# Routing over eleven steps, gate weights written with the last heads' rows, and another split of the opening, in a fused attention and expert kernel

## The chip, the cores and the metric

One core of one Trainium2 chip runs the whole program. The time is device microseconds of one launch; below, us means that. TensorE, VectorE (DVE), ScalarE (ACT), GpSimd (POOL) and SyncE (SP, which issues most DMAs) run in parallel, each with its own queue of instructions in program order, and wait for each other by semaphores.

## What is computed

Attention over 4 batches, 8 heads, 576 tokens and 64 dimensions, a mixture of 8 experts with one expert per token, and a gated feed-forward layer, all in float32:

```python
q_rot, k_rot = rotate(q), rotate(k)                      # rotary positions
scores = q_rot @ k_rot.T / 8                             # 32 heads of 576 x 576
attn = exp(scores - max); attn /= sum(attn) + 1e-9
x = (attn @ v).transpose(0, 2, 1, 3).reshape(2304, 512)
logits = x @ w_gate                                      # 8 experts
e = argmax(logits); gate_w = softmax(logits)[e]
eom = sigmoid(x @ w_output_gate)[e]
x = gate_w * eom * (relu(x @ w1[e]) @ w2[e])
out = (sigmoid(x @ g) * (x @ v2)) @ o                    # 512 -> 1536 -> 512
```

## The kernel before

The program has three stages: attention with routing (0 to about 360 us), the experts (to about 656 us) and the feed-forward layer (to the end). Each float32 operand of a large matmul is split into an upper half (rounded) and a lower half (the rest), and three products are added.

**Attention** works on 16 pairs of heads, g = 0 to 15, four pairs to a batch, and each pair takes five steps j = 0 to 4 of 128 query rows (the last step of 64). The step counter is t = 5g + j. The order of the work is written out by hand in one loop: a step issues `scores(t)` on TensorE, row maxima (L274) on DVE and exponentials (L281) on ScalarE, then the products with v of step t-2, the transposes of the probabilities of step t-1, and parts of the work for other pairs:

- `rot(g, nm)` rotates queries or keys of a pair: part `a` is three products, part `b` the sum. The pair is rotated two pairs ahead, on GpSimd, in steps 0, 1 (`a`) and 3, 4 (`b`). Pair 0 is rotated on DVE. For pair 1, GpSimd makes the products and DVE the sums, in steps 2 and 3 of pair 0.
- `tqk(g)` transposes what was rotated and splits it into halves, one pair ahead, in steps 0 (keys), 1 (queries) and 2 (the 64 last tokens, `tails`); the halves are made on DVE.
- `xf(g)` in steps 3 and 4 transposes the result of pair g-1, divides it by the row sums (tile `x`), makes the pair's part of the logits (tile `lh`) and writes the rows to `x_dram` through SP's queue (L390, L393).
- `load(g+3)`, in step 4, queues the next loads of q, k and v on SP.

**Routing.** When a batch's four pairs are through, `route(b)` returns seven lists of small operations, and the loop runs one list per step, from the step after `xf` of the last pair: logits summed over the eight heads, maximum, one-hot of the first maximum, positions by small matmuls with a triangular matrix, a scatter of token numbers to `perm_dram` by five indirect DMAs on GpSimd (`scatter`), and the gate weight `den`, which goes to column 512 of `x_dram`, one float to a row. For batches 0 to 2 this lies beside the attention of the next pairs; for batch 3 the operations are placed by hand between the first experts' matmuls. After batch 2, `slots(False)` computes a table of which expert takes which rows: 23 small operations on DVE, five to a step. At t = 75 the first experts' weights and rows are loaded (`load_w`, `gather`).

Of the kernel before, what the change touches and what calls it, by code (L numbers as in the profile page):

```python
# [9 lines left out]
F32 = mybir.dt.float32  # L10
# [33 lines left out]
XW = DM + 1  # L44
# [20 lines left out]
def tile_kernel(  # L65
# [60 lines left out]
    pp = pool(att_a, "pp", 3)  # L126
    ptp = pool(att_a, "ptp", 3)
    per = pool(att_a, "per", 1)
    xp = pool(att_a, "xp", 2)
    sm = pool(att_a, "sm", 8)  # L130
    rt = pool(att_a, "rt", 1)
    qkt = pool(att_q, "qkt", 1)
# [77 lines left out]

        return a, b

    def tqk(g):
        i = g % 2

        def halves_of(hi, lo, ps, nm):

            f = SCALE if nm == "q" else 1.0
            nc.vector.tensor_scalar(out=hi, in0=ps, scalar1=f, scalar2=None, op0=ALU.mult)
            nc.vector.scalar_tensor_tensor(  # L220
                out=lo, in0=ps, scalar=f, in1=hi.bitcast(F32), op0=ALU.mult, op1=ALU.subtract
            )

        def main(nm):
            def f():
                src = rotd[g, nm]
                h, l = qT[i] if nm == "q" else (t[:, 64:576] for t in kT[i])
                ps = pst.tile([128, 512], F32, tag="t", name="t")
                for c in range(4):
                    nc.tensor.transpose(ps[:, 128 * c : 128 * c + 128], src[:, c, :], idf)  # L230
                halves_of(h, l, ps, nm)

            return f

        def tails():
            ps = pst.tile([128, 512], F32, tag="t", name="t")
            for n, nm in enumerate("kq"):
                nc.tensor.transpose(ps[:, 64 * n : 64 * n + 64], rotd.pop((g, nm))[0:64, 4, :], idf[0:64, 0:64])
            for c in (0, 576):
                halves_of(*(t[:, c : c + 64] for t in kT[i]), ps[:, 0:64], "k")  # L240
            for e in range(2):
                r = slice(64 * e, 64 * e + 64)
                halves_of(*(t[r, r] for t in qD[i]), ps[r, 64:128], "q")

        return [main("k"), main("q"), tails]
# [96 lines left out]

    def xf(g):
        b, h = divmod(g, 4)
        l = lsum[b % 2][:, :, 2 * h : 2 * h + 2]
        st = {}

        def part(c0, nch):  # L350
            def f():
                if c0 == 0:
                    st["r"] = sm.tile([128, 5, 2], F32, tag="r", name="r")
                    st["x"] = xp.tile([128, 5, 128], F32, tag="x", name="x")
                    sp = sm.tile([128, 2], F32, tag="sp", name="sp")
                    nc.vector.tensor_tensor(out=sp, in0=halves, in1=lst.pop(g).to_broadcast([128, 2]), op=ALU.mult)
                    st["sp"] = sp
                X, r = st["x"], st["r"][:, c0 : c0 + nch, :]
                ps = pst.tile([128, 512], F32, tag="t", name="t")
                for c in range(nch):  # L360
                    cc = c0 + c
                    nc.tensor.matmul(
                        ps[:, 160 * c : 160 * c + 160],
                        O[g % 2][:, 128 * cc : 128 * cc + 128],
                        wI[:, h, :],
                        start=True,
                        stop=True,
                    )
                if c0:
                    nc.tensor.matmul(ps[:, 320:322], fold, st["sp"], start=True, stop=True)  # L370
                    nc.vector.tensor_copy(l[:, 4, :], ps[:, 320:322])
                nc.vector.tensor_scalar(out=r, in0=l[:, c0 : c0 + nch, :], scalar1=EPS, scalar2=None, op0=ALU.add)
                nc.vector.reciprocal(out=r, in_=r)
                r = r.unsqueeze(3)
                pv_ = ps[:, 0 : 160 * nch].rearrange("p (c w) -> p c w", w=160)
                nc.vector.tensor_tensor(
                    out=lh[:, c0 : c0 + nch, 2 * h : 2 * h + 2, :],
                    in0=pv_[:, :, 128:160].rearrange("p c (e w) -> p c e w", e=2),
                    in1=r.to_broadcast([128, nch, 2, 2 * E]),
                    op=ALU.mult,  # L380
                )
                nc.vector.tensor_tensor(
                    out=X[:, c0 : c0 + nch, :].rearrange("p c (e d) -> p c e d", e=2),
                    in0=pv_[:, :, 0:128].rearrange("p c (e d) -> p c e d", e=2),
                    in1=r.to_broadcast([128, nch, 2, D]),
                    op=ALU.mult,
                )
                if c0:
                    t0, hc = b * S + 1, slice(128 * h, 128 * h + 128)
                    nc.sync.dma_start(  # L390
                        out=x_dram[t0 : t0 + 512, hc].rearrange("(p c) d -> p c d", c=4), in_=X[:, 0:4, :]
                    )
                    nc.sync.dma_start(out=x_dram[t0 + 512 : t0 + 576, hc], in_=X[0:64, 4, :])  # L393

            return f

        return [part(0, 3), part(3, 2)]
# [11 lines left out]
    def route(b):  # L409
# [4 lines left out]
        def logits():  # L414
            st["lg"] = lg = t3("lg", 2 * E)
            st["L"] = lg[:, :, 0:E]
            nc.vector.tensor_reduce(out=lg, in_=lh.rearrange("p c h e -> p c e h"), axis=AX.X, op=ALU.add)

        def top():
            st["mx"] = t2("mx")  # L420
# [93 lines left out]

        def weight():
            den = st["den"]
            nc.vector.reciprocal(out=den, in_=den)
            t0 = b * S + 1
            nc.sync.dma_start(
                out=x_dram[t0 : t0 + 512, DM : DM + 1].rearrange("(p c) d -> p (c d)", c=4), in_=den[:, 0:4]  # L520
            )
            nc.sync.dma_start(out=x_dram[t0 + 512 : t0 + 576, DM : DM + 1], in_=den[0:64, 4:5])

        return [
            [logits, top, at_top],
            [first, first_max, onehot],
            [before],
            [place, own, own_sum],
            [scatter, gate],
            [gate_sum, guard, both],  # L530
            [weight],
        ]

    def scatter_group(ins, b, c):
# [430 lines left out]
    for nm in "kq":  # L965
        for f in R[nm]:
            f(eng=nc.vector)
    first = tqk(0)
    first[0]()
    first[1]()  # L970
    first[2]()
    load(2)
    second = {nm: rot(1, nm) for nm in "kq"}
    for nm in "kq":
        second[nm][0]()

    def late_setup():
        nc.sync.dma_start(out=mc, in_=misc)
# [36 lines left out]
    for t in range(NJ * NPAIR):  # L1015
        g, j = divmod(t, NJ)
        if t == NJ * (NPAIR - 1):
            att_b.close()
            open_moe()
            M["table"], M["later"], M["ids"], M["want"] = False, [], 0, FRONT  # L1020
            more_ids()
            for i in range(NPC):
                load_w(0, i)
            gather(0)
            gather(1)
        scores(g, j)
        if t >= 2:
            pv(*divmod(t - 2, NJ))
        if t >= 1:
            turn_last(*divmod(t - 1, NJ))  # L1030
        if g >= 1 and j in (3, 4):
            if j == 3:
                xs_ = xf(g - 1)
            xs_[j - 3]()
        if g == 0:
            if j == 2:
                tq = tqk(1)
                second["k"][1](nc.vector)
                tq[0]()
            elif j == 3:  # L1040
                second["q"][1](nc.vector)
                tq[1]()
            elif j == 4:
                tq[2]()
        elif g + 1 < NPAIR and j < 3:
            if j == 0:
                tq = tqk(g + 1)
            tq[j]()
        if t >= 1:
            turn(*divmod(t - 1, NJ))  # L1050

        n = g + 2
        if n < NPAIR:
            if j == 0:
                ahead[n] = rot(n, "k"), rot(n, "q")
                ahead[n][0][0]()
            elif j == 1:
                ahead[n][1][0]()
            elif j == 3:
                ahead[n][0][1]()  # L1060
            elif j == 4:
                ahead.pop(n)[1][1]()
                if g + 3 < NPAIR:
                    load(g + 3)
        if t == 2:
            late_setup()
        if t == 5:
            late_setup2()
        if j == 4 and g >= 4 and g % 4 == 0:
            for n, fs in enumerate(route(g // 4 - 1)):  # L1070
                plan.setdefault(t + 1 + n, []).extend(fs)
            if g == NPAIR - 4:
                it = iter(slots(False))
                for n in range(5, 10):
                    plan.setdefault(t + n, []).extend(islice(it, 5))
                plan[t + 10] = list(it)
        for f in plan.pop(t, []):
            f()
        if g == NPAIR - 1 and j in (2, 3):
            take(1)  # L1080
# [237 lines left out]
```

## Time and profile before

| | |
|---|---|
| median of 3 runs | 1150.48 us (1150.36 to 1151.25) |
| profiled execution, own time | 1141.22 us |
| its span, first to last instruction | 1139.5 us |
| TensorE busy | 1074.9 us, 94% of the span |
| DVE, ScalarE, GpSimd busy | 68%, 51%, 30% |
| mean granted TensorE clock | 0.985 of full speed |

The span is that of one execution under the hardware profiler. Busy shares are averages over the three stages; matmuls are pipelined, so that a busy TensorE isn't one at its peak. Timeline rows give the start, the duration, the engine, the source line, the operation, the tiles (out<-in), and in brackets the idle time of the engine before it with what ended that.

### The profile page before, as it was taken

Reading aid. Unit: us, or ns where it says so; the run is one execution under the profiler, and the core shown is the slowest. Engines: PE = TensorE matmul, PEld = TensorE weight load, DVE = VectorE, ACT = ScalarE, POOL = GpSimd, SP = SyncE. Lnnn points to the kernel's source line nnn. Section 1 sums busy time; section 2 is a strip of 40 time slices with the busy share of each in tenths; the row PEclk is TensorE's granted clock in tenths of the full one; section 3 lists DMA queues with packets and bytes.
Section 4 is the critical chain, followed back from the end, with each engine's and each line's share of the span. In section 5 each row is a group of like instructions: output and inputs, shape, how many; then the busy total and the mean of one; then the engine's idle time right before and its main releaser. Section 6 shows DMA issues by size and latency. Waiting matters only on the chain. (4 is left out here: it accounts for less than half of the span.)

```text
span 1139.5 us, 20624 instructions
## 1 busy us (share of the span) xinstructions
PE 1074.9 (94%) x7644; PEld 960.6 (84%) x7644; DVE 774.7 (68%) x1450; ACT 581.5 (51%) x1116; POOL 343.8 (30%) x324
## 2 busy tenths in 40 slices
PE   4999899889999999999999998899999999999998
PEld 3788788768778988887988887789999999999997
DVE  6878787768876887788888678864454444545442
ACT  2566466446554345566667455644443444444442
POOL 3636356353612213332224044521111111111111
PEclk9999899889999999999999999899999999999999
DMA  3132162144107396789999425310010010100000
GB/s 110 37 83 44 43 84 44 43 43 85 43 16 220 56 193 217 231 291 307 296 307 310 145 79 191 112 56 1 1 56 1 1 57 1 56 1 1 28 1 28
DMA packets 99485, 111.61 MB, mean 98 GB/s; under 512 B 19249, under 2 KB 77873, under 8 KB 99378
## 3 DMA queue, kind: packets, MB, share of 16 engines
q1 hardware_dynamic: 94914, 97.81, 31.0%
q0 software_dynamic: 4320, 12.08, 3.4%
q8 instruction: 62, 1.02, 0.4%
q10 hardware_dynamic: 144, 0.33, 0.1%
q14 instruction: 45, 0.37, 0.1%
HBM read 103.03 MB, written 15.56 MB: 104 GB/s over the span
## 5 line engine op out<-in xcount | busy, mean ns | idle before, releaser
L1202 POOL TENSOR_TENSOR gl<-gf,gh 128x384 fp32r<-128x384 f32 x72 | 73.1, 1015 | 350.9 <-ACT gh L1201 350.9
L281 ACT ACTIVATE p<-s,nm 128x576 f32<-128x576 f32 x144 | 105.5, 737 | 133.8 <-DVE nm L274 131.7
L746 DVE TENSOR_TENSOR lo<-wr,hi 128x1024 fp32r<-128x1024 f32 x112 | 150.4, 1359 | 17.8 <-ACT hi L745 17.4
L1198 DVE TENSOR_TENSOR gf<-v,sg 128x384 f32<-128x384 f32 x72 | 39.9, 554 | 138.6 <-PE v L1194 138.6
L274 DVE TENSOR_REDUCE nm<-s 128x1 f32<-128x576 f32 x144 | 102.9, 751 | 39.0 <-PE s L268 26.0
L1180 DVE TENSOR_TENSOR gl<-gw,gh 128x512 fp32r<-128x512 f32 x72 | 73.5, 1021 | 68.9 <-ACT gh L1179 68.9
L1201 ACT CAST gh<-gf 128x384 fp32r<-128x384 f32 x72 | 36.9, 513 | 161.6 <-DVE gf L1198 161.6
L745 ACT CAST hi<-wr 128x1024 fp32r<-128x1024 f32 x106 | 109.5, 1052 | 4.2 <-PE y L836 2.8
L1192 PE MATMUL t<-yh,gh 128*128 128x384 f32 x288 | 100.4, 349 | 6.7 <-ACT sg L1196 5.8
L1194 PE MATMUL t<-yh,gl 128*128 128x384 f32 x288 | 99.0, 344 | 4.1 <-DVE gl L1180 4.1
L314 PE MATMUL t<-idf,p 128*128 128x128 f32 x576 | 83.5, 280 | 18.6 <-DVE pt L300 16.2
L1193 PE MATMUL t<-yl,gh 128*128 128x384 f32 x288 | 98.2, 341 | 0.0
L1192 PE MATMUL v<-yh,vh 128*128 128x384 f32 x288 | 96.6, 335 | 0.0
L1193 PE MATMUL v<-yl,vh 128*128 128x384 f32 x288 | 96.5, 335 | 0.0
L1194 PE MATMUL v<-yh,vl 128*128 128x384 f32 x288 | 96.4, 335 | 0.0
L317 ACT COPY pt<-t 128x512 f32<-128x512 f32 x144 | 79.1, 588 | 32.9 <-PE t L314 32.1
L314 PEld LDWEIGHTS t<-idf,p 128*128 128x128 f32 x576 | 66.2, 145 | 24.9 <-DVE pt L300 20.5
L1216 PE MATMUL o<-oh,gl 128*128 128x512 f32 x216 | 86.2, 399 | 0.0
L1215 PE MATMUL o<-ol,gh 128*128 128x512 f32 x216 | 85.3, 395 | 0.0
L1214 PE MATMUL o<-oh,gh 128*128 128x512 f32 x216 | 84.0, 389 | 0.0
L805 PE MATMUL h<-xl,hi 128*128 128x256 f32 x288 | 82.0, 285 | 1.7 <-DVE sc L781 1.7
L805 PE MATMUL h<-xh,hi 128*128 128x256 f32 x288 | 81.9, 284 | 0.7 <-issue 0.7
(218 smaller groups left out, 2890.2 us busy)
## 6 DMA issues: line engine op xcount, KB each, us to landing
wr<-in_moe_w_dram SPq DMA_DIRECT2D x112, 512.0 KB
cv<-in_moe_w_gate_dram SPq DMA_DIRECT2D x12, 512.0 KB
cv<-in_moe_w_val_dram SPq DMA_DIRECT2D x12, 512.0 KB
cv<-in_moe_w_out_dram SPq DMA_DIRECT2D x12, 512.0 KB
yt<-y_dram SPq DMA_DIRECT2D x18, 256.0 KB
out_dram<-ob SPq DMA_DIRECT2D x18, 256.0 KB
kraw<-in_k_dram SPq DMA_DIRECT2D x16, 256.0 KB
qraw<-in_q_dram SPq DMA_DIRECT2D x16, 256.0 KB
```

Of the source, the lines that this page charges most:

```text
L274: nc.vector.tensor_reduce(out=nm, in_=s[:, :, 0:288], axis=AX.XY, op=ALU.max, negate=True)
L281: nc.scalar.activation(out=P[g, j][:, e, :].rearrange("p (a b) -> p a b", a=2), in_=s[:, :, 0:288], func=AF.Exp, bias=nm, scale=1.0, accum ...
L314: nc.tensor.transpose(ps[:, 128 * c : 128 * c + 128], src[:, e, k0 + 128 * c : k0 + 128 * c + 128], idf)
L745: nc.scalar.copy(out=hi, in_=t)
L746: nc.vector.tensor_tensor(out=lo, in0=t, in1=hi.bitcast(F32), op=ALU.subtract)
L805: nc.tensor.matmul(ps[:, c, :], w[:, kk, 128 * c : 128 * c + 128], x[:, kk, :], start=first, stop=last)
L1192: nc.tensor.matmul(ps[:, 0:TG], wh[:, c], yh[:, kk, :], start=(kk == 0), stop=False)
L1193: nc.tensor.matmul(ps[:, 0:TG], wh[:, c], yl[:, kk, :], start=False, stop=False)
L1194: nc.tensor.matmul(ps[:, 0:TG], wl[:, c], yh[:, kk, :], start=False, stop=(kk == KD - 1))
L1214: nc.tensor.matmul(ps, gh[:, c], wh, start=(f == 0), stop=False)
L1215: nc.tensor.matmul(ps, gh[:, c], wl, start=False, stop=False)
L1216: nc.tensor.matmul(ps, gl[:, c], wh, start=False, stop=(f == NF - 1))
```

## The change

Five things change.

- The opening: the upper halves of pair 0 are made on ScalarE; TensorE runs 30 transposes of the identity ahead of the keys' transposes and 8 ahead of the queries', into the same PSUM tile. GpSimd copies one element of the rotated queries before it starts on pair 1, and makes pair 1's sums as well.
- For batches 0 to 2 the sum over heads is made by three adds on GpSimd instead of one reduction on DVE.
- `route` returns eleven lists instead of seven, and the first runs in the step of `xf` itself, one step earlier than before.
- The table's operations come six to a step, from the step after `place`.
- The rows of a batch's last pair are kept (tile `x` has three buffers and a 129th column) until the gate weight is there, and rows and weight are written together, 129 columns wide.

```diff
-    xp = pool(att_a, "xp", 2)
+    xp = pool(att_a, "xp", 3)
...
-    def tqk(g):
+    def tqk(g, eng=nc.vector, spin=(0, 0, 0)):
         i = g % 2
+        def place(n):
+            ps = pst.tile([128, 512], F32, tag="t", name="t")
+            for _ in range(spin[n]):
+                nc.tensor.transpose(ps[:, 0:128], idf, idf)
+            return ps
...
-            nc.vector.tensor_scalar(out=hi, in0=ps, scalar1=f, scalar2=None, op0=ALU.mult)
+            if eng is nc.scalar:
+                nc.scalar.activation(out=hi, in_=ps, func=AF.Copy, scale=f)
+            else:
+                nc.vector.tensor_scalar(out=hi, in0=ps, scalar1=f, scalar2=None, op0=ALU.mult)
...
+    xlast = {}
+    def put_x(X, b, hc):
+        t0, w = b * S + 1, hc.stop - hc.start
+        nc.sync.dma_start(
+            out=x_dram[t0 : t0 + 512, hc].rearrange("(p c) d -> p c d", c=4), in_=X[:, 0:4, 0:w]
+        )
+        nc.sync.dma_start(out=x_dram[t0 + 512 : t0 + 576, hc], in_=X[0:64, 4, 0:w])
...
-                if c0:
...
+                if c0 and h < 3:
+                    put_x(X, b, slice(128 * h, 128 * h + 128))
+                elif c0:
+                    xlast[b] = X
...
-            nc.vector.tensor_reduce(out=lg, in_=lh.rearrange("p c h e -> p c e h"), axis=AX.X, op=ALU.add)
+            if b == B - 1:
+                nc.vector.tensor_reduce(out=lg, in_=lh.rearrange("p c h e -> p c e h"), axis=AX.X, op=ALU.add)
+                return
+            s4 = rt.tile([128, 5, 4, 2 * E], F32, tag="s4", name="s4")
+            s2 = rt.tile([128, 5, 2, 2 * E], F32, tag="s2", name="s2")
+            for o, x, n in ((s4, lh, 4), (s2, s4, 2), (lg.unsqueeze(2), s2, 1)):
+                nc.gpsimd.tensor_tensor(out=o, in0=x[:, :, 0:n, :], in1=x[:, :, n : 2 * n, :], op=ALU.add)
...
-            nc.vector.reciprocal(out=den, in_=den)
...
+            X = xlast.pop(b)
+            nc.vector.reciprocal(out=X[:, :, 128], in_=den)
+            put_x(X, b, slice(384, XW))
...
-            [logits, top, at_top], [first, first_max, onehot], [before], [place, own, own_sum],
-            [scatter, gate], [gate_sum, guard, both], [weight],
+            [logits], [top, at_top], [first, first_max], [onehot], [before], [place],
+            [own, own_sum], [scatter], [gate], [gate_sum], [guard, both, weight],
...
-    first = tqk(0)
+    first, gate_q = tqk(0, nc.scalar, (30, 8, 0)), rotd[0, "q"]
...
+    nc.gpsimd.tensor_copy(scr, gate_q[0:1, 0, 0:1])
     load(2)
     second = {nm: rot(1, nm) for nm in "kq"}
     for nm in "kq":
-        second[nm][0]()
+        for f in second[nm]:
+            f()
...
-                second["k"][1](nc.vector)
...
-                second["q"][1](nc.vector)
...
-                plan.setdefault(t + 1 + n, []).extend(fs)
+                plan.setdefault(t + n, []).extend(fs)
...
-                for n in range(5, 10):
-                    plan.setdefault(t + n, []).extend(islice(it, 5))
-                plan[t + 10] = list(it)
+                for n in range(6, 11):
+                    plan.setdefault(t + n, []).extend(islice(it, 6))
+                plan[t + 10] += list(it)
```

## Rows read from the trace of the kernel before

**Rows 1.** The page: busy time by engine, and one of the costliest groups.

```profile
PE 1074.9 (94%) x7644; PEld 960.6 (84%) x7644; DVE 774.7 (68%) x1450; ACT 581.5 (51%) x1116; POOL 343.8 (30%) x324
...
L317 ACT COPY pt<-t 128x512 f32<-128x512 f32 x144 | 79.1, 588 | 32.9 <-PE t L314 32.1
```

**Rows 2.** Busy time by stretch: from, to, length; busy per engine; clock; DMA.

```profile
79.29:118.14 38.85, 38.46 (x420) 33.04 (x416) 30.73 (x81) 23.74 (x55) 18.74 (x16) 1.00 0.29 63
118.14:164.91 46.77, 42.74 (x440) 36.12 (x436) 37.85 (x100) 24.06 (x57) 22.27 (x24) 0.93 0.37 50
203.71:257.08 53.37, 44.61 (x440) 37.72 (x436) 37.42 (x100) 23.98 (x56) 23.80 (x25) 0.87 0.33 44
295.91:341.78 45.87, 41.74 (x440) 35.23 (x436) 38.29 (x123) 23.95 (x56) 14.49 (x17) 0.96 0.15 34
```

**Rows 3.** Timeline of the opening, to the first exponential.

```profile
6.14 0.89 DVE L199 TENSOR_TENSOR tb<-kraw,ropes 128x320 f32<-128x320 f32 x2
...
7.06 0.83 DVE L207 TENSOR_TENSOR trk<-ta,tb 128x640 f32<-128x640 f32 x1
...
8.04 1.09 PE L230 MATMUL t<-idf,trk 128*128 128x128 f32 x4 [8.04 <-DVE trk L207]
...
8.54 2.23 DVE L199 TENSOR_TENSOR tb<-qraw,ropes 128x320 f32<-128x320 f32 x2
8.66 1.75 POOL L192 TENSOR_TENSOR ta<-kraw,ropes 128x640 f32<-128x640 f32 x1 [6.34 <-DMA kraw<-in_k_dram]
...
10.80 1.36 DVE L207 TENSOR_TENSOR trq<-ta,tb 128x640 f32<-128x640 f32 x1
...
12.08 0.68 DVE L219 TENSOR_SCALAR kTh<-t 128x512 fp32r<-128x512 f32 x1
...
16.24 0.23 DVE L220 SCALAR_TENSOR_TENSOR qDl<-t,qDh 64x64 fp32r<-64x64 f32 x1
...
17.43 0.74 ACT L281 ACTIVATE p<-s,nm 128x576 f32<-128x576 f32 x1 [14.91 <-DVE nm L274]
```

**Rows 4.** Timeline of the opening, TensorE's wait for pair 1's keys.

```profile
27.07 0.63 PE L230 MATMUL t<-idf,trk 128*128 128x128 f32 x4 [1.33 <-DVE trk L207]
```

**Rows 5.** Timeline of batch 0's routing, DVE and GpSimd.

```profile
120.85 1.23 DVE L417 TENSOR_REDUCE lg<-lh 128x80 f32<-128x640 f32 x1
...
122.34 0.20 DVE L425 TENSOR_TENSOR val<-lg,mx 128x40 f32<-128x40 f32 x1
...
127.02 1.53 POOL L192 TENSOR_TENSOR ta<-qraw,ropes 128x640 f32<-128x640 f32 x1
...
127.04 1.57 DVE L443 TENSOR_TENSOR d<-lg,mx 128x40 f32<-128x40 f32 x1
```

**Rows 6.** Timeline of an ordinary pair and the next one's start, by engine.

```profile
105.52 1.54 POOL L192 TENSOR_TENSOR ta<-kraw,ropes 128x640 f32<-128x640 f32 x1 [10.53 <-DMA kraw<-in_k_dram]
...
109.06 1.42 DVE L274 TENSOR_REDUCE nm<-s 128x1 f32<-128x576 f32 x2 [0.26 <-PE s L268]
...
111.82 1.57 POOL L207 TENSOR_TENSOR trk<-ta,tb 128x640 f32<-128x640 f32 x1
...
116.56 0.58 SPq L390 DMA_DIRECT2D x_dram<-x  x1
...
118.75 0.60 PE L230 MATMUL t<-idf,trk 128*128 128x128 f32 x4
```

**Rows 7.** Timeline of GpSimd, first and last of batch 0's five scatters.

```profile
143.57 1.14 POOL L485 DMA_INDIRECT perm_dram<-ids_tok,pi  x1 [10.38 <-DVE tmp L497]
...
148.81 0.90 POOL L485 DMA_INDIRECT perm_dram<-ids_tok,pi  x1 [0.22 <-issue]
```

**Rows 8.** Timeline of batch 1's second routing pair, DVE and GpSimd.

```profile
242.84 1.42 DVE L274 TENSOR_REDUCE nm<-s 128x1 f32<-128x576 f32 x2 [5.32 <-remote]
...
247.09 1.53 POOL L192 TENSOR_TENSOR ta<-kraw,ropes 128x640 f32<-128x640 f32 x1 [11.70 <-DMA kraw<-in_k_dram]
```

**Rows 9.** Timeline of DVE at the first experts' weights.

```profile
350.66 0.91 DVE L743 CAST hi<-wr 128x1024 fp32r<-128x1024 f32 x1 [0.85 <-DMA wr<-in_moe_w_dram]
```

More of the change, by code (lines that the diff above doesn't have):

```diff
@@ L227, in f @@
                 h, l = qT[i] if nm == "q" else (t[:, 64:576] for t in kT[i])
-                ps = pst.tile([128, 512], F32, tag="t", name="t")
+                ps = place("kq".index(nm))
                 for c in range(4):
@@ L235, in tails @@
         def tails():
-            ps = pst.tile([128, 512], F32, tag="t", name="t")
+            ps = place(2)
             for n, nm in enumerate("kq"):
@@ L353, in f @@
                     st["r"] = sm.tile([128, 5, 2], F32, tag="r", name="r")
-                    st["x"] = xp.tile([128, 5, 128], F32, tag="x", name="x")
+                    st["x"] = xp.tile([128, 5, 129], F32, tag="x", name="x")
                     sp = sm.tile([128, 2], F32, tag="sp", name="sp")
@@ L382, in f @@
                 nc.vector.tensor_tensor(
-                    out=X[:, c0 : c0 + nch, :].rearrange("p c (e d) -> p c e d", e=2),
+                    out=X[:, c0 : c0 + nch, 0:128].rearrange("p c (e d) -> p c e d", e=2),
                     in0=pv_[:, :, 0:128].rearrange("p c (e d) -> p c e d", e=2),
@@ L387, in f @@
                 )
-                if c0:
[L389 to L393, printed above, removed]
+                if c0 and h < 3:
+                    put_x(X, b, slice(128 * h, 128 * h + 128))
+                elif c0:
+                    xlast[b] = X
             return f
@@ L516, in weight @@
             den = st["den"]
-            nc.vector.reciprocal(out=den, in_=den)
[L518 to L522, printed above, removed]
+            X = xlast.pop(b)
+            nc.vector.reciprocal(out=X[:, :, 128], in_=den)
+            put_x(X, b, slice(384, XW))
         return [
-            [logits, top, at_top],
-            [first, first_max, onehot],
+            [logits],
+            [top, at_top],
+            [first, first_max],
+            [onehot],
             [before],
[L528 to L531, printed above, removed]
+            [place],
+            [own, own_sum],
+            [scatter],
+            [gate],
+            [gate_sum],
+            [guard, both, weight],
         ]
@@ L967, in tile_kernel @@
             f(eng=nc.vector)
-    first = tqk(0)
-    first[0]()
-    first[1]()
-    first[2]()
+    first, gate_q = tqk(0, nc.scalar, (30, 8, 0)), rotd[0, "q"]
+    for f in first:
+        f()
+    nc.gpsimd.tensor_copy(scr, gate_q[0:1, 0, 0:1])
     load(2)
@@ L974, in tile_kernel @@
     for nm in "kq":
-        second[nm][0]()
+        for f in second[nm]:
+            f()
     def late_setup():
```

## The prediction

> **What bounds the kernel now.** The page comes first: TensorE is busy for 94% of the span [rows 1], so a microsecond is won where TensorE waits or runs at half clock. The busy table by stretch says where that is: two ordinary pairs of heads last 38.85 us, with TensorE busy for 38.46; the two pairs that hold the routing of batch 0 last 46.77, those of batch 1 53.37, those of batch 2 45.87, at mean granted clocks of 0.93, 0.87 and 0.96 [rows 2]. That is 7.9, 14.5 and 7.0 us too much, 29.4 together. The timeline of the first 34 us shows the other place: the first exponential starts at 17.43 [rows 3], and later TensorE waits twice for rotated keys and queries of pair 1 [rows 4]. In the routing's timeline the reader is to see a DVE instruction that lasts as long as a GpSimd one [rows 5], in that of an ordinary pair who waits in the queues of SP and GpSimd, and how little room DVE has [rows 6]: scores(t+1) waits for the exponentials of step t, these for the row maxima on DVE, and in the third step of a pair DVE is idle for only 0.26 us before the maxima. DVE work beyond some tenths per step reaches TensorE.
>
> **The opening.** DVE's rotation of pair 0's queries runs against GpSimd's product for pair 1, started at 8.66: its two half products take 2.23 where the same two for the keys took 0.89, its sum 1.36 where that of the keys took 0.83 [rows 3]. With GpSimd gated until the queries are done, 0.89 and 0.83 hold for both: trq is ready at 10.3 instead of 12.16. Behind it DVE had twelve upper and lower halves, four of 0.68 and eight of 0.2, to 16.47 [rows 3]. The upper halves move to ScalarE, idle then, where a 128x512 copy out of PSUM takes 0.59 [rows 1]. The new chain: trq 10.3; four transposes 0.6 to 1.1 (at either clock, rows 6 and 3); upper half 0.6; lower half 0.7; four small lower halves 0.9: 13.1 to 13.6. The first exponential comes 1.0 after the last half, as before (16.47 to 17.43), and I allow 0.2 for semaphores: 14.3 to 14.8. Worth 2.6 to 3.1, taken 2.9.
>
> The thirty spin transposes cost nothing while they end before trk (7.9). They start when the identity is written, at about 2.4; at 1.09 for four, 1.2 GHz [rows 3], they would last to 10.6, at 0.60, 2.4 GHz [rows 6], to 6.9. If the clock rises on the way they end about 8.5: the keys are a little late, but have slack until trq. At the slow end the queries' eight spins (2.2) come on top, and the opening loses up to 2.5.
>
> Pair 1's sums move from DVE to GpSimd: per tensor 1.54 + 1.7 + 1.57 [rows 6] (the two half products together as long as the whole one and a little), 9.6 for both, from 10.3 to 20, before step 2 reads them (about 22). So the wait of 1.33 [rows 4], one of two, the other 1.34, goes: 2.7. Next late is step 5's set-up on DVE, unchanged. Opening: -2.9 - 2.7 = **-5.6**, bounds -2.5 and -7.
>
> **Routing: what goes.** The sum over heads, 1.23, leaves DVE for three batches [rows 5]. On GpSimd, adds of 320, 160 and 80 elements at 1.54 per 640 [rows 6] are 1.35, with their starts up to 2. They begin when the last logits are written (just before the row write of 116.56) and GpSimd's rotation is over (trk ends at 113.39, trq 1.55 later) [rows 6]; top reads them a step later: hidden. After that DVE gets some 0.4 us of routing per step, two instructions of 0.20 [rows 5], where three to six stood together.
>
> **Routing: what it meets.** DVE's subtraction of two SBUF tiles took 1.57, from 127.04 to 128.61, beside GpSimd's product of 127.02 to 128.55; the like comparison at 122.34, with GpSimd idle, took 0.20 [rows 5]. So a two-input step costs 0.2, or up to 1.55 if it starts under a rotation. The Trainium skill (GPSIMD Engine Reference, Specifications) says that GpSimd's SBUF interfaces are shared with VectorE and contended by DVE instructions with two SBUF inputs. The trace agrees: 1.57 against 0.20.
>
> Where will the rotation be? SP stood at the row write until 116.56, with the next pair's loads queued behind it [rows 6]. In the pair after a batch's last head no row write stands there, so that load runs most of a pair earlier, and GpSimd rotates right behind its adds, from 118 to 127.5. at_top and first fall under it, the one-hot steps no longer. In the second routing pair the load is as late as ever: GpSimd starts 6.8 after the pair's start (105.52 against 98.7, half of 38.85 before 118.14), and tmp falls under the queries' product.
>
> Sum per batch, in excess of two ordinary pairs: top and at_top 0.4 + 0.7 of port wait; first and first_max 0.4 + 0.8 less 0.4 of slack; one-hot 0.2 beyond slack; the twenty 8-column matmuls and oh 1.0 (estimate: 0.05 each, under the 0.15 of a 128-column transpose in rows 6); place 0; own 0.3; index 0; tmp 1.1; gate sums 0.3; weight 0: 4.4, and 0.5 for what clock is still lost: **4.9**. The port waits are 0 to 1.55 for each of three to five steps: bounds 2.2 and 8.
>
> The scatter, five indirect DMAs of 6.2 us together (143.57 to 149.71) [rows 7], now stands in GpSimd's queue between the queries' products and the sums. It puts the end of trk from 14.7 after the pair's start to 20.9; TensorE reads trk at 20.0 [rows 6], and 1.7 later in a pair so much longer: 0.8 to spare. Without that delay it costs 0.9.
>
> Batch 0: 7.9 to 4.9, **-3.0**. Batch 1 has one thing more: from 237.5 DVE starts nothing for 5.32 us, and no releaser is known; the keys' product starts 16.5 instead of 6.8 after the pair's start (247.09 against 230.6) [rows 8]. The scatter was issued beside that pair's row write and loads; now it is issued ahead of the next ones and is nearly over when they start. I count as gone the 5.3 and 1.5 of the half clock behind it (the clock's deficit, 0.13 x 53.4 = 6.9, is 3.6 more than batch 0's): 14.5 to 4.9, **-9.6**. Batch 2: no rotation in its second pair, so tmp costs 0.2, but the table's 23 small DVE steps come six to a step instead of five: 7.0 to 5.5, **-1.5**.
>
> **The last heads' rows.** 516-byte rows replace 512-byte rows and four-byte writes; nobody waits for them until the gather. For batch 2 two row DMAs (0.58 [rows 6] each and a little) now stand in SP's queue ahead of the first experts' weights, for which DVE already waits 0.85 [rows 9]: **+1.2**, bounds 0 and 2.5. At the tail the last rows move into a busier stretch of DMA: +0.3, bounds -1 and 2.
>
> **Sum.** -5.6 - 3.0 - 9.6 - 1.5 + 1.5 = -18.2 against the profiled execution's 1141.22 (span 1139.5): 1123.0. The median of the timed runs, 1150.48, is 9.3 above that execution, so I carry over the difference, not the level. Whether the timed runs contain the hold of 5.32 can't be read; without it and its clock the sum is -11.4. Between the two I take -14.5: **1136.0 us**.
>
> **Rivals.**
> *Stalls move rather than go.* By the shared interface, five two-input steps at 1.55 are 7.8 a batch, and the routing costs what it did. For: the 1.57 of rows 5. Against: by the order above only one or two fall under each rotation. Left are -5.6 + 1.5 = -4.1: 1146.4. Chance 0.17.
> *The scatter holds the next loads: slower.* If it drags into them, keys land 9.7 late as in rows 8; 5.4 of that (118.75 - 113.39) is slack, so 4.3 per batch, with hold and half clock 11.1. For both batches: -18.2 + 22.2 = +4.0, 1154.5. It decides only if both have it; with one the kernel stays faster. For: the five DMAs did it once in two. Against: they are issued about 5 us earlier against the loads. Chance 0.07.
> *The opening doesn't do what it says.* The spins run at 1.2 GHz throughout and hold the transposes: it gives 3.1 instead of 5.6, 1138.5. Chance 0.11.
>
> **Numbers.** The forecast has 0.65. Range 1128 to 1147: from -18.2 with 4 of the lower bounds added, up to the first rival; it leaves out the slower rival and the tails. Less than 0.2%, 2.3 us, can't be told from no change. Faster 0.87, same 0.05, slower 0.08: the slower rival, and a little of the first.
>
> **What would show it.** Right: first exponential at 14 to 15, no wait for trk or trq of pair 1; routing pairs of 43 to 45 us for two at a clock near 1; GpSimd's rotation directly behind its adds in the first of them. Wrong: spins still running at 8.5; two-input steps of 1.5 in four places of a batch; TensorE waiting for trk behind the scatter; DVE waiting over 2 us for the first experts' weights.

## The result and the profile after

| | median us | lowest to highest | runs |
|---|---|---|---|
| before | 1150.87 | 1150.36 to 1153.59 | 4 |
| after | 1140.49 | 1137.66 to 1141.25 | 4 |

Ratio 0.990, 95% interval 0.988 to 0.992: the changed kernel is faster by 10.4 us. The forecast was 14.5 (1136.0 us, with a range of 1128 to 1147, in which 1140.49 lies). But the two profiled executions differ by 1.2 us only: spans 1139.5 and 1138.3, own times 1141.22 and 1140.11. In both, the last exponential of attention starts at 358.6: what the routing won there was lost again in the opening and in other pairs. The profile of after agrees with its timed runs; that of before took 9.7 us less than the median of its own. The experiments had to settle where the change wins and loses, and what the level of the timed runs is made of.

The page of after: busy time per engine, and the copy of [rows 1].

```profile
PE 1074.3 (94%) x7682; PEld 958.8 (84%) x7682; DVE 771.9 (68%) x1439; ACT 583.7 (51%) x1122; POOL 353.1 (31%) x336
...
L327 ACT COPY pt<-t 128x512 f32<-128x512 f32 x144 | 79.5, 589 | 33.2 <-PE t L324 26.4
```

Nothing is to be seen there: TensorE is as busy as in [rows 1]. Busy time by stretch of after, as in [rows 2]: two ordinary pairs, the routing pairs of batches 0, 1 and 2, and the first stretch to pair 2.

```profile
61.84:100.65 38.81, 38.41 (x420) 33.00 (x416) 30.81 (x81) 23.76 (x55) 18.75 (x16) 1.00 0.30 63
120.06:166.62 46.56, 42.38 (x452) 35.42 (x448) 37.72 (x99) 23.97 (x56) 24.05 (x26) 1.00 0.20 33
207.80:254.04 46.24, 41.69 (x434) 35.25 (x436) 35.86 (x99) 23.87 (x57) 24.66 (x27) 0.97 0.13 27
293.14:340.50 47.36, 41.41 (x440) 34.10 (x436) 36.49 (x122) 24.07 (x56) 14.81 (x18) 1.00 0.04 9
14.90:61.84 46.94, 39.76 (x378) 33.88 (x378) 32.70 (x74) 23.17 (x54) 24.82 (x25) 0.85 0.12 29
```

Above the ordinary 38.8, the batches cost 7.8, 7.4 and 8.6 us; before it was 7.9, 14.5 and 7.0 [rows 2], forecast were 4.9, 4.9 and 5.5. Batch 1 is shorter by 7, the others are not. The opening begins nearly as forecast: the first exponential starts 2.5 us earlier than in [rows 3]. Here are the last upper half on ScalarE and that exponential:

```profile
13.60 0.22 ACT L227 ACTIVATE qDh<-t 64x64 fp32r<-64x64 f32 x1 [0.28 <-DVE qDl L230]
...
14.90 0.74 ACT L291 ACTIVATE p<-s,nm 128x576 f32<-128x576 f32 x1 [1.08 <-DVE nm L284]
```

Pair 1 then starts at 34.55 (39.49 before), 4.9 earlier, and pair 2 at 61.84 (59.87), 2.0 later. The reader finds the loss in steps 5 to 7: step 5 lasts 9.52 us where it lasted 4.51, and the next two are 1.2 and 1.0 longer, with a granted clock of 0.50 in the first of them. This is step 5, DVE first, then GpSimd, then TensorE:

```profile
37.68 1.70 DVE L1020 COPY wI<-idf 128x512 f32<-128x512 f32 x1
39.30 0.87 DVE L1021 CAST tri<-mc 128x128 bf16<-128x128 f32 x1
40.10 2.38 DVE L1023 TENSOR_TENSOR fold<-idf 128x64 f32<-128x64 f32 x2
...
42.54 0.70 DVE L1027 CAST ids_tok<-mc 128x20 int32<-128x20 f32 x1
...
43.23 1.41 DVE L284 TENSOR_REDUCE nm<-s 128x1 f32<-128x576 f32 x2
```

```profile
37.56 1.54 POOL L192 TENSOR_TENSOR ta<-kraw,ropes 128x640 f32<-128x640 f32 x1 [7.22 <-DMA kraw<-in_k_dram]
39.06 1.84 POOL L199 TENSOR_TENSOR tb<-kraw,ropes 128x320 f32<-128x320 f32 x2
40.87 1.53 POOL L192 TENSOR_TENSOR ta<-qraw,ropes 128x640 f32<-128x640 f32 x1
```

```profile
45.35 0.90 PE L324 MATMUL t<-idf,p 128*128 128x128 f32 x3 [6.17 <-DVE pt L310]
```

Each of the set-up's copies and additions lasts to about the end of the GpSimd instruction that it meets; the row maxima wait behind them, and TensorE is idle for 6.17. In the kernel before, the set-up ran ahead of GpSimd's rotation (DVE, then GpSimd):

```profile
42.20 0.41 DVE L994 COPY wI<-idf 128x512 f32<-128x512 f32 x1
```

```profile
45.73 1.56 POOL L192 TENSOR_TENSOR ta<-kraw,ropes 128x640 f32<-128x640 f32 x1 [6.14 <-DMA kraw<-in_k_dram]
```

A like collision stands at the end of the second routing pair of batches 0 and 1. In batch 0 it holds DVE's product for the weights; GpSimd's sums are below it:

```profile
161.76 0.16 DVE L530 TENSOR_SCALAR den<-den 128x5 f32<-128x5 f32 x1
162.03 3.64 DVE L534 SCALAR_TENSOR_TENSOR den<-zs,den 128x5 f32<-128x5 f32 x1
165.70 0.19 DVE L541 RECIPROCAL x<-den 128x5 f32<-128x5 f32 x1
```

```profile
161.67 0.90 POOL L508 DMA_INDIRECT perm_dram<-ids_tok,pi  x1 [0.23 <-issue]
162.59 1.55 POOL L207 TENSOR_TENSOR trk<-ta,tb 128x640 f32<-128x640 f32 x1
164.09 1.54 POOL L207 TENSOR_TENSOR trq<-ta,tb 128x640 f32<-128x640 f32 x1
```

Five elements per partition take 3.64 us, to the end of both sums, which the scatter had made late. That step lasts 7.62 instead of 4.2. In batch 1 the like step lasts 7.60, but there the product takes 0.17. DVE is idle for 3.59 us while the scatter is issued, with no releaser known, and then an addition that belongs to `xf` is held to the end of the second sum (251.9):

```profile
249.93 0.29 DVE L310 COPY pt<-t 128x128 f32<-128x128 f32 x1 [3.59 <-remote]
...
250.32 1.61 DVE L391 TENSOR_SCALAR r<-lsum 128x4 f32<-128x4 f32 x1
```

### The profile page after: what moved, and what is told of

Read it like the earlier page. It is cut to its first block, busy times and chain, and to the rows that moved or that the text cites. A ratio compares the mean times of both kernels' runs of the same rounds, so it can differ in the third digit from the quotient of the medians.

```text
span 1138.3 us, 20687 instructions
## 1 busy us (share of the span) xinstructions
PE 1074.3 (94%) x7682; PEld 958.8 (84%) x7682; DVE 771.9 (68%) x1439; ACT 583.7 (51%) x1122; POOL 353.1 (31%) x336
```

## The experiments

Three chips were used: the first four runs on one, the next four on another, the last four on a third; which chip ran the pair of the result is not on record. The kernel before ran beside each four: 1139.08 (29 runs, 1134.8 to 1143.6), 1139.08 (22 runs, 1134.3 to 1147.7) and 1145.38 (23 runs, 1140.3 to 1152.8). So only kernels of one chip are compared in us, and the ratios to before across chips. A ratio is estimated from all the runs and is not quite the quotient of the medians.

| | median us | ratio to before | 95% interval |
|---|---|---|---|
| e1_before | 1139.10 | 1.000 | 0.998 to 1.003 |
| e2_opening | 1141.45 | 1.002 | 1.000 to 1.004 |
| e3_routing | 1133.85 | 0.997 | 0.994 to 0.999 |
| e4_setup4 | 1128.78 | 0.992 | 0.990 to 0.995 |
| e5_after | 1134.55 | 0.997 | 0.995 to 0.999 |
| e6_weight11 | 1131.25 | 0.993 | 0.990 to 0.995 |
| e7_both | 1122.56 | 0.986 | 0.983 to 0.989 |
| e8_defer | 1129.77 | 0.992 | 0.990 to 0.995 |
| e9_nospin | 1134.42 | 0.989 | 0.986 to 0.993 |
| e10_dvelogits | 1139.31 | 0.994 | 0.992 to 0.997 |
| e11_bothdefer | 1130.24 | 0.987 | 0.983 to 0.990 |
| e12_open4 | 1140.19 | 0.995 | 0.992 to 0.997 |

### e1_before: the kernel before once more

No edit.

> The kernel before, unchanged, profiled a second time and timed against itself. Its first profiled execution took 1141.22 us of its own, 9.7 below the median of its timed runs (1150.87). Theory: the held transfers, which in that execution kept back one late reduction on VectorE by 5.3 us in batch 1 alone, come in most executions in more than one batch, so that the new profile shows a longer span, with a hold of 4 to 6 us in batch 0 or batch 2 as well, or a longer one in batch 1; own time 1145 to 1153. Rival one: the first profile shows all that there is and profiling itself makes this kernel 9 to 10 us shorter; then the new one is again at 1139 to 1143, with the same rows, and its timed runs at 1150 to 1151. Rival two: the difference lies in the experts' part, in which the weights arrive; then the pairs start as in the first profile and the last pair's first exponential stands at 358.6, and what is behind it is 9 us longer.

The new span is 1144.4, 4.9 longer than the first, and not all stalls lie where they did: batch 1's hold is there again (4.08), the pair behind batch 0's routing has one that the first profile had not, and the first experts' weights are late. The busy table for the three batches, then two rows of DVE:

```profile
117.09:164.07 46.98, 42.68 (x440) 36.30 (x436) 36.63 (x100) 24.05 (x56) 18.27 (x21) 0.93 0.37 50
207.63:261.36 53.73, 45.31 (x440) 38.34 (x436) 38.14 (x100) 23.98 (x56) 23.79 (x25) 0.87 0.31 43
300.21:345.33 45.12, 40.05 (x440) 33.84 (x436) 38.32 (x123) 23.84 (x56) 14.51 (x17) 1.00 0.15 35
```

```profile
168.93 0.69 DVE L219 TENSOR_SCALAR kTh<-t 128x512 fp32r<-128x512 f32 x1 [3.52 <-PE t L230]
...
246.00 1.42 DVE L274 TENSOR_REDUCE nm<-s 128x1 f32<-128x576 f32 x2 [4.08 <-PE t L314]
...
355.99 0.69 DVE L743 CAST hi<-wr 128x1024 fp32r<-128x1024 f32 x1 [2.62 <-DMA wr<-in_moe_w_dram]
```

Keys that come late through GpSimd at 168.93 cost 4.7 (that step lasts 8.29 for 3.55): what the prediction's slower rival feared of the changed kernel, the kernel before has itself, now and then. So stalls vary from execution to execution and the theory holds for the span. It does not explain 1150: on this chip the timed runs are at 1139.1, and this execution is the slowest of its twelve. Rival one is wrong (1146.19 of its own). Rival two is wrong too: 358.6 is the start of attention's last exponential, which now starts at 363.7, and the time behind it is the same within 0.2 us.

### e2_opening: the opening alone

```diff
 # the kernel before, with the opening of the changed one
...
+    first, gate_q = tqk(0, nc.scalar, (30, 8, 0)), rotd[0, "q"]
...
+    nc.gpsimd.tensor_copy(scr, gate_q[0:1, 0, 0:1])
...
-                second["k"][1](nc.vector)
...
-                second["q"][1](nc.vector)
```

> The kernel before with the opening of the changed one alone (the transposes that fill TensorE's wait, ScalarE on the upper halves, GpSimd behind the first pair's rotation, pair 1's sums on GpSimd); routing and weights' rows as before. Theory (the opening's gain is given back in step 5): first exponential at 14.9, pair 1 at 34.5, but the mask set-up on VectorE in step 5 now stands beside GpSimd's rotation of pair 3, its copies take 1.7 us and more, and pair 2 starts at 61.8 where the kernel before has 59.9; the span is 0 to 2.5 us above that of the kernel before in an execution with the same holds; ratio 0.999 to 1.003. Rival (the prediction's sum for the opening): pair 2 starts at 54 to 56, and the ratio is 0.995 to 0.996.

Pair 1 starts at 34.22 and pair 2 at 61.34; the set-up's copy takes 1.68. The time is 2.4 us above before, the ratio 1.002. The theory holds: alone, the opening costs a little. Batch 1's hold is not in this execution, although the routing is the old one: pair 10 lasts 20.1 us.

### e3_routing: routing and rows alone

```diff
 # the changed kernel, with the opening of the kernel before
...
-    first, gate_q = tqk(0, nc.scalar, (30, 8, 0)), rotd[0, "q"]
...
-    nc.gpsimd.tensor_copy(scr, gate_q[0:1, 0, 0:1])
+    first = tqk(0)
...
```

> The changed kernel with the opening of the kernel before: eleven routing steps, the heads' sums on GpSimd and the weights written with the last heads' rows alone. Theory (all that the change brings lies here, and the opening costs 2 us): pair 2 starts at 59.9, batches 0 to 2 as in the changed kernel, one exponential weight product on VectorE held over 3.6 us in batches 0 and 1; time 1137 to 1140, ratio 0.988 to 0.990. Rival (the opening carries part of the gain): time 1143 to 1146, ratio 0.993 to 0.996.

1133.85, 5.2 below before on this chip, 7.6 below e2. Both expectations were written against 1150.9 and miss in level, and the ratio of 0.997 lies above both. In kind the theory holds: the whole gain lies here. Of the two held products one is there: the last step of pair 10 takes 7.41 us, that of pair 6 only 4.17.

### e4_setup4: the mask set-up one step earlier

```diff
-        if t == 5:
+        if t == 4:
             late_setup2()
```

> The changed kernel with one edit: the mask set-up on VectorE (a copy of the identity into the weights, the triangle, the fold, the token numbers) in step 4, where GpSimd has nothing running between 30.3 and 37.6 us, in place of step 5. Theory (the opening's 5 us are lost to the set-up beside GpSimd's rotation): the set-up's operations take their short times (0.2 to 0.4 us each, 1.7 together), pair 1 lasts 20.0 to 21.0 us where it lasts 27.3, pair 2 starts at 54.5 to 56.5, and the time falls by 5 to 7 us, to 1133.5 to 1136. Rival one (TensorE's lower clock behind the opening, not the set-up, makes pair 1 long): pair 2 starts at 60 or later and the time stays within 2 us. Rival two (set-up's inputs, read by a transfer issued in step 2, are not there yet in step 4): VectorE waits in step 4 by as much as is gained.

The same instructions in this trace, with GpSimd idle, where 36.83 is its next start:

```profile
32.85 0.43 DVE L1020 COPY wI<-idf 128x512 f32<-128x512 f32 x1
33.20 0.22 DVE L1021 CAST tri<-mc 128x128 bf16<-128x128 f32 x1
33.33 0.35 DVE L1023 TENSOR_TENSOR fold<-idf 128x64 f32<-128x64 f32 x2
```

Pair 1 lasts 19.29 instead of 27.29 and pair 2 starts at 54.10. The time is 1128.78, 5.1 below e3, which has the old opening and the same routing. One moved line turns the opening from a loss of 2.4 into a gain of 5.1; rivals one and two fall (step 4 itself grows by 0.9). The expected level was written against 1140.5.

### e5_after: the changed kernel on a second occasion

No edit.

> The changed kernel, unchanged, on the chip on which the kernel before is timed beside it. In the first four experiments the kernel before took 1139.1 us there, 11.8 below its median in the runs shown ahead of the prediction, so that the ratio of 0.990 may be of one occasion. Theory: the opening gives back 2.0 (pair 2 at 61.8, for 59.9), the routing brings 5.2 (the kernel with the routing alone took 1133.85), so the changed kernel takes 1135 to 1137 and the ratio is 0.996 to 0.998. Rival (the ratio of the first runs holds anywhere): 1127 to 1129, ratio 0.990.

1134.55, 4.5 below before, ratio 0.997 (0.995 to 0.999): the theory, not the rival. The intervals of the two occasions do not overlap, so the change is worth 10 us on one and 4.5 on the other. Pair 2 starts at 60.32; the batches cost 7.2, 6.6 and 6.7 above the ordinary 38.8. The last steps of pairs 6 and 10 take 7.05 and 6.86. Here it is the addition ahead of the product that is held (3.35 and 3.09), with GpSimd's two sums from 160.24 to 163.30:

```profile
159.98 3.35 DVE L530 TENSOR_SCALAR den<-den 128x5 f32<-128x5 f32 x1
163.44 0.17 DVE L534 SCALAR_TENSOR_TENSOR den<-zs,den 128x5 f32<-128x5 f32 x1
```

### e6_weight11: the weights' last operations one step later

```diff
             [gate_sum],
+            *([[]] if b < 2 else []),
             [guard, both, weight],
```

> The changed kernel with the last three operations of the weights (guard, the two-input product and the reciprocal) one step later in batches 0 and 1, where GpSimd has no sum running. Theory (VectorE's two-input product is held until GpSimd's two sums end): the product takes 0.2 us and not 3.64, the last step of pairs 6 and 10 takes 4.2 us and not 7.6, TensorE's clock does not fall behind it; up to 3.4 us less in each of two batches, less what executions have in which the product already stands clear: 3 to 6 us below the changed kernel. Rival (the product merely ends when something else does, a late semaphore): the last step of pairs 6 and 10 stays at 7 to 8 us and the time stays within 2 us.

The product with GpSimd idle beside it:

```profile
165.62 0.17 DVE L534 SCALAR_TENSOR_TENSOR den<-zs,den 128x5 f32<-128x5 f32 x1
```

The last steps of pairs 6 and 10 take 4.15 and 4.16, and the time is 3.3 below e5 on the same chip. Away from GpSimd's sums neither the product nor the addition ahead of it is held (0.17 and 0.16): the theory, not the rival.

### e7_both: both moves

```diff
-        if t == 5:
+        if t == 4:
             late_setup2()
...
+            *([[]] if b < 2 else []),
             [guard, both, weight],
```

> The changed kernel with the mask set-up in step 4 and the weights' last operations one step later, together. Theory (two separate collisions of VectorE with GpSimd): the two gains add up, 3 to 5 us below the kernel with the set-up moved alone (1128.78), so 1124 to 1126, ratio to the kernel before 0.987 to 0.989. Rival (what the second edit frees is taken by the loads that come late behind the scatter of token numbers): 1127 to 1129.

1122.56, 12.0 below e5 on the same chip and ratio 0.986: faster than both kernels, and below what was expected. Its batches:

```profile
112.55:155.65 43.10, 40.47 (x440) 34.04 (x436) 34.50 (x96) 23.75 (x57) 22.43 (x25) 1.00 0.17 31
196.49:238.81 42.32, 40.05 (x436) 33.97 (x436) 33.95 (x96) 23.70 (x57) 23.19 (x27) 1.00 0.15 31
279.81:324.13 44.32, 40.46 (x440) 34.04 (x436) 36.20 (x122) 23.75 (x56) 14.47 (x18) 1.00 0.04 10
```

They cost 4.3, 3.5 and 5.5 above 38.8, where the prediction had 4.9, 4.9 and 5.5.

### e8_defer: no scatter beside the loads of batches 0 and 1

```diff
-            for c in range(5):
+            for b2 in ([], [], [0, 1, 2], [3])[b]:
+                for c in range(5):
 ...             # indirect_dma_start as before, with pis[b2]
```

> The changed kernel with the token numbers of batches 0 and 1 scattered in batch 2, ahead of its own, so that no scatter runs in pairs 5 to 12 beside loads; nothing is left out. Theory (the stalls of 1 to 5 us that fall on other steps in each execution come from loads and events that are late behind the 4-byte scatter): pairs 6, 7, 10 and 11 last 19.4 to 20.5 us each with no step above 5.2, the last step of pairs 6 and 10 is short as well, because GpSimd's sums run in their usual place; batch 2 (pairs 13 to 15) gets longer by 3 to 12 us for ten more scatters of 1.25 us each; the span from pair 5 to pair 12 falls from 153.7 to 142 to 146. Rival (the stalls come from elsewhere): steps of 5.5 to 8 us are still found in pairs 6, 7, 10 or 11.

```profile
119.95:163.13 43.18, 40.56 (x440) 34.08 (x436) 35.14 (x99) 23.88 (x56) 18.77 (x17) 1.00 0.16 31
201.96:244.85 42.89, 40.25 (x440) 34.03 (x436) 34.85 (x99) 23.87 (x56) 18.78 (x17) 1.00 0.14 31
283.67:331.68 48.01, 43.06 (x440) 36.32 (x436) 36.17 (x122) 23.94 (x57) 25.04 (x38) 0.93 0.05 10
```

Pairs 6, 7, 10 and 11 last 20.2, 19.4, 19.9 and 19.4, no step is above 4.5, and from pair 5 to pair 12 it is 144.3 (152.0 in e5). Of the 7.7 us, 5.6 come from the last steps of pairs 6 and 10, where GpSimd's sums now run early and hold nothing (4.17 each), and 2.4 from pairs 7 and 11. Batch 2 gets 2.5 longer. The time is 4.8 below e5. The theory holds: stalls in these pairs come with the scatter, whether by GpSimd's time or by DMA; the two are not told apart here.

### e9_nospin: e7 without the spin transposes

```diff
-    first, gate_q = tqk(0, nc.scalar, (30, 8, 0)), rotd[0, "q"]
+    first, gate_q = tqk(0, nc.scalar, (0, 0, 0)), rotd[0, "q"]
```

> The kernel with both moves (mask set-up in step 4, weights' last operations one step later; 1122.56 us) without the transposes that fill TensorE's wait in the opening. Theory (they raise the granted clock for the opening's own transposes and scores): the four transposes of k take 1.1 us and not 0.66, first exponential at 15.5 to 16.0 and not 14.8, pair 1 starts 0.6 to 1.2 us later, time 1123 to 1124. Rival (the work brought forward brings forward a stretch of half clock too: in the changed kernel one of 6.8 us began at 15.5, and the kernel before had none there): the first exponential is later by 0.7 but pair 1 starts at the same time within 0.3 us, and the time is the same.

The four transposes of the keys take 1.09 instead of 0.60 and the first exponential starts at 15.17 (14.79 in e7), but pair 1 starts at 35.00 (35.01) and pair 2 at 54.30 (54.31). So the rival: the spins are worth 0.4 us for one step, nothing behind it. (The expected time was written against e7's chip.) The ratios of e7 and e9 (0.986, 0.989) overlap and are of different chips. On this third chip a hold of e5's kind is back, in a kernel that had moved its weights: the last steps of pairs 6 and 10 take 7.40 and 8.05 (4.16 in e7). Now it strikes an instruction of `xf` in the same step. Pair 6, DVE, then GpSimd:

```profile
154.53 0.16 DVE L390 COPY lsum<-t 128x2 f32<-128x2 f32 x1 [1.12 <-PE t L324]
154.72 2.61 DVE L391 TENSOR_SCALAR r<-lsum 128x4 f32<-128x4 f32 x1
```

```profile
154.24 1.57 POOL L207 TENSOR_TENSOR trk<-ta,tb 128x640 f32<-128x640 f32 x1
155.75 1.55 POOL L207 TENSOR_TENSOR trq<-ta,tb 128x640 f32<-128x640 f32 x1
```

DVE reached this place 1.65 us later than in e7 (154.53, there 152.88), and so GpSimd's sums, at the same time in both, caught an addition of four elements. Why DVE was late is not shown; the scatter was being issued until 154.2 in both. The move of the weights takes two instructions out of the sums' way, and leaves the sums where they meet others.

### e10_dvelogits: e7 with the heads' sum back on DVE

```diff
-            if b == B - 1:
-                nc.vector.tensor_reduce(out=lg, ...)
-                return
-            ...                                  # three additions on GpSimd
+            nc.vector.tensor_reduce(out=lg, ...)
```

> The kernel with both moves, with the heads' gate values summed in all batches by one reduction on VectorE, as in the kernel before, and not by three additions on GpSimd. Theory (VectorE stands in the chain of each step, so its 1.23 us there count): the first step of pairs 5, 9 and 13 takes 4.7 to 5.2 us and not 4.0, the time rises by 2 to 4 us to 1124.5 to 1126.5. Rival (VectorE has room in that step, or the additions delay GpSimd's rotation by as much): the time stays within 1 us of 1122.56.

1139.31, 4.9 above e9 on the same chip (they differ by the spins too, which cost nothing). The step that grows (the first of pairs 5 and 9, 5.84 and 5.89 for 4.04; that of pair 13 takes 4.34) does so by what follows the reduction. The reduction itself, 1.26, runs in the step before, where the row maxima of pair 5 start only 0.08 us later than in e9:

```profile
114.90 0.18 DVE L438 TENSOR_REDUCE mx<-lg 128x5 f32<-128x40 f32 x1
115.12 2.56 DVE L442 TENSOR_TENSOR val<-lg,mx 128x40 f32<-128x40 f32 x1
```

```profile
114.58 1.54 POOL L207 TENSOR_TENSOR trk<-ta,tb 128x640 f32<-128x640 f32 x1
116.09 1.53 POOL L207 TENSOR_TENSOR trq<-ta,tb 128x640 f32<-128x640 f32 x1
```

Without its additions GpSimd rotates earlier, its sums meet the first comparison, and that is held for 2.56 (0.35 in e9, where the first sum starts at 118.86). The theory's direction is right, its reason half wrong: the additions on GpSimd gain also because they shift the rotation past a DVE instruction.

### e11_bothdefer: both moves and the deferred scatter

Edits of e7 and e8 together.

> The kernel with both moves, and the scatters of token numbers of batches 0 and 1 put into batch 2 ahead of its own. Theory (the edits are independent): pairs 7 and 11 lose the 1.9 to 2.2 us that late loads still cost there, batch 2 gets 3 to 4 us longer; time 1121 to 1124, near that of the kernel with both moves, with a smaller spread. Rival (without the scatter GpSimd's sums run earlier and meet the weights' operations in their new place): pairs 6 and 10 above 21 us and 1125 or more.

1130.24 on the third chip, ratio 0.987; 4.2 below e9. Batches 0 and 1 cost 4.5 and 3.9 above 38.8 (7.6 and 7.9 in e9). Batch 2, with fifteen indirect DMAs, lasts 53.55, 9.2 more than in e7: what is deferred is paid for in part, and the theory had 3 to 4 us for it. Pairs 6 and 10 stay at 20.3 and 19.8, so the rival falls. In ratio it equals e7, with lowest and highest 4.1 apart (e9: 7.7).

### e12_open4: opening and moved set-up on the kernel before

The edits of e2 and e4 together.

> The kernel before with the opening of the changed one and the mask set-up in step 4; routing and weights' rows as before. Theory (the opening is worth what the prediction gave it, 5.6 us, once the set-up does not stand beside GpSimd's rotation): pair 2 at 54.0 to 54.5, time 1133 to 1135 where the opening alone gave 1141.45 and the kernel before 1139.1; ratio 0.994 to 0.996. Rival (what the opening frees is taken by the late loads of the batches): 1137 to 1140.

1140.19, 5.2 below before on this chip, ratio 0.995, pair 2 at 54.00: theory. (The level was written against 1139.) The old routing's stalls lie elsewhere again in this execution: batches cost 11.3, 10.6 and 11.0 above 38.8, where e1 had 8.2, 14.9 and 6.3. One of them, which begins as the last of the five indirect DMAs is issued (140.88):

```profile
143.36 1.42 DVE L284 TENSOR_REDUCE nm<-s 128x1 f32<-128x576 f32 x2 [2.54 <-remote]
```

## Why the prediction was right, and where its steps were not

**The level.** 14.5 was taken, 10.4 and 4.5 were measured on two occasions. The sum of the terms, -18.2, was never reached; e7, with two moves more, came to -16.5. That 10.4 lies near 14.5 is in part luck: the opening, forecast at -5.6, cost 2.4 (e2), the two profiled executions differ by 1.2 only, and the timed runs of before on that occasion lay 5.5 to 11.8 us above those on the three chips, for a reason that stays open.

**Opening, -5.6.** The first exponential (14.90, just beyond 14.3 to 14.8), the waits for pair 1 (gone) and the spins (over at 7.3; in e7 at 8.5, with the keys 0.3 later) were nearly right. With the set-up out of the way the size was too: -5.1 (e4 against e3) and -5.2 (e12). What failed is the sentence "Next late is step 5's set-up on DVE, unchanged". The set-up was unchanged; its neighbour was not. Before, GpSimd's rotation of pair 3 began at 45.7, behind the set-up; in the changed kernel it began at 37.56, on top of it, and the gain became a loss of 2.4 (e2). That start moved by 8.2 us and not by the 4.9 of pair 1: GpSimd waits there for a load, and SP issued the loads of pair 3 9.3 us earlier.

**Batches 0 and 2, -3.0 and -1.5.** The terms of the sum per batch add up to 4.8 and not to 4.4, so with the 0.5 for the clock it should read 5.3. The first routing pair of batch 0 shrank from 26.7 to 23.0 us (in e5, e7 and e9 alike). GpSimd's rotation stood right behind its additions (120.07) and tmp took the 1.12 forecast for it. The failed step is "weight 0": the last operations of the weights were priced without the scatter that delays GpSimd's sums into them, though the prediction had put trk behind the scatter one paragraph on. One of them is held for 3.1 to 3.7 us in batch 0 of after, in both batches of e5, and in batch 1 of e3 and e4; in batch 0 of e3 and e4 none is. With them moved, batches 0 and 1 cost 4.3 and 3.4 (e6) and 4.3 and 3.5 (e7), below the summed 4.9, but 7.6 and 7.9 in e9, where the sums caught another instruction. Batch 2 has no such sums. It cost 8.6 in after, 6.7 in e5, and the forecast 5.5 in e4 and e7; with the old routing it was 7.0, 6.3 (e1), 9.9 (e2) and 11.0 (e12). Where its stalls come from is open.

**Batch 1, -9.6.** The 5.3 of hold was counted as gone because the scatter is issued earlier. With the old routing e1 has it again (4.08), but e2 has not: the forecast rested on a stall that comes and goes. With the new routing e5 has none, while in after one of 3.59, without a known releaser either, stands at the end of the same pair (249.93). Batch 1 cost 7.4 and 6.6 there, for the 4.9 forecast. In e4 stalls of 2 to 3 us stand in the pairs behind (a step of 6.81 in pair 7 and of 5.83 in pair 11, both 3.82 in e8), and e8 and e11 show that they go when the scatter goes. So the term was right in direction, but part of it is spread and not removed.

**First experts' weights, +1.2.** DVE waits 2.31 in after, 0.85 in [rows 9]; that looks like the term. But e1 waits 2.62, e2 3.04 and e12 1.51, all with the rows written the old way, and the other changed kernels 1.9 to 2.5. The term is not shown; 0.85 was the short end of a spread.

**Rivals.** "Stalls move rather than go" was the nearest: as a mechanism it was right in two places (the opening's set-up and the weights), and its 1146.4, -4.1 against its 1150.48, is what the second occasion measured (-4.5). Against it the prediction held that only one or two two-input steps fall under a rotation; the count was about right, but copies and additions with one input are held as well, and a hold can span two sums. The Trainium skill (GPSIMD Engine Reference, Specifications) names DVE's 2-port mode beside two SBUF inputs; the prediction used the second half only. The traces agree that two inputs are not needed: the set-up's copy, with one, took 1.70 beside GpSimd and 0.43 without (e4). Which mode it ran in no trace shows.

**Open.** Why before took 1150.9 on the first occasion, and 1139.1, 1139.1 and 1145.4 later: no execution of it at 1150 was profiled. That the stalls of one kernel differ between executions is seen (the first profile of before against e1); whether they differ by chip, and whether they make up the 11 us, is not shown.

## What to carry to other kernels

When an edit starts an engine earlier, list what the other engines run at the new time, also unchanged set-up work: here one line (`t == 4`) was worth 7.5 us (from +2.4 to -5.1). Price a small DVE instruction between SBUF tiles by the GpSimd instructions that may run beside it, not by its size, and put it where GpSimd waits for a load. Profile the kernel before twice ahead of a forecast that rests on one stall.

## What the runs showed of the hardware

- DVE's hold beside GpSimd need not end with one GpSimd instruction: 3.64, 3.35, 2.61 and 2.56 us reached to the end of two back-to-back sums (1.55 and 1.54). It can end with one: in e10 a comparison begun at 293.45 took 1.06, to the end of the first sum, while the second followed at once. What decides between the two is not shown. Reductions from SBUF (0.18 at 114.90, beside a sum) and instructions that read PSUM (kTl, qTl: 0.69 throughout) were not held.
- TensorE's duration and its granted clock need not agree. In after, TensorE had been idle for 2.26 us when step 1's scores began at 15.79; a pair of them took 0.67, and the granted clock of 15 to 19 reads 0.56 (1.2 GHz for most of it). In e9, without spins and idle for 1.75, the same pair took 0.68 where that window's granted clock reads 1.00 (2.4 GHz); later in both pairs take 0.29 to 0.30.
- The same kernel's medians were 1139.1, 1139.1 and 1145.4 on three chips, and 1150.9 on the occasion of the result.
